# Two score regions for a group of two pairs in place of three, the third score tile in two banks of the MoE pool

## Chip, cores and metric

One core of one Trainium2 chip. The metric is the device time in microseconds (us) of one execution; every ratio compares fast runs alone (an execution over 1.5% above the fastest of its kernel counts as slow); medians and ranges are of all runs. "Span" is the profiled time from the first to the last instruction, some 2 us less than the time. Data are bf16 on chip, with float32 inputs, outputs and PSUM sums.

## The reference, cut to what matters

```python
# q, k, v: (8 batches, 8 heads, 576 positions, 64)
scores = (q @ k.transpose(0, 1, 3, 2)) / 8
scores = where(pos_i // 64 >= pos_j // 64, scores, -1e9)   # blockwise causal
attn = softmax(scores) @ v
x = attn.transpose(0, 2, 1, 3).reshape(4608, 512)
return maximum(x @ w1, x @ w2) @ w_out                      # d_ff = 1024
```

Two heads are a *pair* (32 in all), two pairs a *group* (16).

## The kernel before: the parts that matter

The program is written by hand in order, engine by engine. TensorE works on 128 rows of its array for the hidden matmuls (`ps_h`), the output matmuls (`ps_y`) and attention times values (`ps_o`), and on 64 rows for transposes and scores. A *region* is a stretch of 64-row work between stretches of 128-row work. TensorE's results land in the tiles of the PSUM pools, which the program lays out in *banks*: a bank here is the room of one `ps_m` tile of 128x512 float32. A tile's bank is used again once VectorE or ScalarE has copied the tile out (*evicted* it): at 24.33 us of the trace before, the first transpose into `ps_xo`, whose bank held the first `ps_kT` tile, starts 0.05 us after VectorE's copy of that tile has ended. The pools take eight banks: `ps_s` has two tiles of two banks for scores, `ps_m` four tiles of one bank for all else. It is called the MoE pool after the feed-forward part, whose first two products are the *hidden* matmuls and whose last one is the *output*; a *unit* is what fills and empties one tile of output, or a pair of hidden tiles.

```python
ps_s = ctx.enter_context(tc.tile_pool(name="ps_s", bufs=2, space=bass.MemoryType.PSUM))
ps_m = ctx.enter_context(tc.tile_pool(name="ps_m", bufs=4, space=bass.MemoryType.PSUM))

def h_unit(i, f):                    # 4 matmuls into each of two banks, then a maximum
    ...
    for w_sb in (w1_sb, w2_sb):
        pt = ps_m.tile([P, SPAN], FP32, name="ps_h", tag="m")
        for c in range(NDM):
            nc.tensor.matmul(pt[:, :w], w_sb[:, c, f * P:(f + 1) * P], xT[:, c, t0:t0 + w], ...)
            if c == NDM - 1:
                if not ph:
                    nc.vector.tensor_copy(out=h1[:, :w], in_=pt[:, :w])
                else:
                    nc.vector.tensor_max(g[:, f, m:m + w], h1[:, :w], pt[:, :w])
    ...
def transposes(nm, g, copies):       # two banks of ps_m, emptied by VectorE and ScalarE
    pts = [ps_m.tile([P, RPP, NP], BF16, name=f"ps_{nm}T", tag="m") for _ in range(2)]
    ...
def tile_0(p):                       # one of three score tiles of a pair, one exp
    u = ps_s.tile([P, 2, 512], FP32, name="ps_s", tag="s")
    scores(p, u, 0, 0, 0, 512)
    return lambda: (exp(p, u, 512, 0), mask(p, 0))
    ...
def x_out(g, t0=0, t1=NCH):          # transposes a group's x through two banks of ps_m
    pe = ps_m.tile([P, 2, n, BLK], BF16, name="ps_xe", tag="m")
    po = ps_m.tile([P, 2, n_odd, BLK], BF16, name="ps_xo", tag="m")
    ...
    nc.vector.tensor_copy(out=dst[:, :, :, 0], in_=pe[:])
    nc.vector.tensor_copy(out=dst[:, :, :n_odd, 1], in_=po[:])
    ...
for g in range(GPB, NG):             # fill(n): the next n hidden or output matmuls
    a, b = 2 * g, 2 * g + 1
    if x_due:
        x_out(x_due.pop())
    region(tile_0(a), tile_1(a))
    ...
    for p, tiles in ((a, lambda: (tile_2(a), tile_0(b))), (b, lambda: (tile_1(b), tile_2(b)))):
        fill(hi)
        av_with(p - LAG, lo)
        copy_out = t_pair(p)         # q's transposes of the next group with a, k's with b
        outs = tiles()
        copy_out()
        region(*outs)
        ...
```

The softmax here doesn't subtract the row's maximum and nothing guards it: scores larger than these inputs give would overflow.

## Time and profile before

| | before |
|---|---|
| time, median of 3 runs | 283.12 us (282.26 to 705.16; the last is not a fast run) |
| span, granted clock | 280.4 us, 1.000 |
| busy: TensorE, VectorE, ScalarE, GpSimd | 96, 66, 50, 38% |
| regions in a steady group, row-size changes in all | 3, 122 |
| steady group, between the starts of two x transposes | 15.0 us |

For later comparison I split the trace where each group's x transposes begin. For each stretch, *content* is the TensorE work that no wait explains: each 128-row matmul at the spacing seen when nothing waits (0.216 us for 512 columns), two 64-row ones on different halves of the array side by side, 0.094 us for each change of row size (92 to 97 ns in the steady groups). The *remainder* is the length less the content. A steady group before has 14.76 us of content and 0.25 of remainder.

### The profile page before, as it was taken

Reading aid. Unit: us, or ns where it says so; the run is one execution under the profiler, and the core shown is the slowest. Engines: PE = TensorE matmul, PEld = TensorE weight load, DVE = VectorE, ACT = ScalarE, POOL = GpSimd, SP = SyncE. Lnnn points to the kernel's source line nnn. Section 1 sums busy time; section 2 is a strip of 40 time slices with the busy share of each in tenths; the row PEclk is TensorE's granted clock in tenths of the full one; section 3 lists DMA queues with packets and bytes.
Section 4 is the critical chain, followed back from the end, with each engine's and each line's share of the span. In section 5 each row is a group of like instructions: output and inputs, shape, how many; then the busy total and the mean of one; then the engine's idle time right before and its main releaser. Section 6 shows DMA issues by size and latency. Waiting matters only on the chain.

```text
span 280.4 us, 7767 instructions
## 1 busy us (share of the span) xinstructions
PE 269.3 (96%) x3208; PEld 151.5 (54%) x3253; DVE 185.7 (66%) x386; ACT 139.6 (50%) x194; POOL 107.7 (38%) x271
## 2 busy tenths in 40 slices
PE   7699999999999999999999999999999999999995
PEld 2356766655556455555555554646455644444543
DVE  5967879668887676767667576757655766365430
ACT  3786577667664664655647374664653000100112
POOL 2996446764654625164344625371120000000000
PEclk9999999999999999999999999999999999999999
DMA  7999999979934994479266866175301111111114
GB/s 261 263 219 220 187 244 273 250 148 189 210 42 153 154 156 78 178 82 239 49 208 77 219 75 196 52 81 50 67 5 49 49 54 40 39 75 40 73 41 150
DMA packets 55940, 36.68 MB, mean 131 GB/s; under 512 B 38752, under 2 KB 43232, under 8 KB 55904
## 3 DMA queue, kind: packets, MB, share of 16 engines
q0 software_dynamic: 41728, 7.87, 35.0%
q1 hardware_dynamic: 13760, 27.66, 28.8%
q10 hardware_dynamic: 416, 0.66, 0.7%
q8 instruction: 25, 0.41, 0.6%
q14 instruction: 11, 0.09, 0.1%
HBM read 34.60 MB, written 9.44 MB: 157 GB/s over the span
## 4 chain that ended last, share of the span: by engine, by line
PE 91%; DMA 4%; issue 2%; ACT 1%; DVE 1%; POOL 0%; ACTq 0%
PE ps_h L197 43%; PE ps_y L215 22%; PE ps_o L429 11%; PE ps_s L321 8%; DMA vv<-in_v_dram 2%; PE ps_xe L451 2%; PE ps_qT L303 2%; DMA qraw<-in_q_dram 2%; PE ps_kT L303 2%; ACT aT L345 1%; PE ps_s L339 1%; PE ps_y L231 1%; PE ps_w L292 1%; DVE g L206 0%; POOL vv L133 0%
## 5 line engine op out<-in xcount | busy, mean ns | idle before, releaser
L197 PE MATMUL ps_h<-xT,w_sb 128*128 128x512 bf16 (+3 forms) x605 | 136.2, 357 | 1.7 <-issue 0.3
L345 ACT ACTIVATE aT<-ps_s 128x1024 bf16<-128x1024 f32 (+2 forms) x100 | 96.2, 996 | 17.2 <-PE ps_s L321 16.2
L197 PEld LDWEIGHTS <-w_sb 128*128 128x128 bf16 x640 | 57.8, 98 | 57.4 <-issue 8.1
L204 DVE CAST h<-ps_h 128x512 bf16<-128x512 f32 (+3 forms) x80 | 50.9, 637 | 28.9 <-PE ps_h L197 26.7
L215 PE MATMUL ps_y<-wo_sb,g 128*128 128x512 bf16 x273 | 65.5, 379 | 2.1 <-PE ps_s L321 1.3
L206 DVE TENSOR_TENSOR g<-h,ps_h 128x512 bf16<-128x512 bf16 (+3 forms) x80 | 50.6, 632 | 12.0 <-PE ps_h L197 10.5
L350 POOL MEMSET aT<- 64x128 bf16 x124 | 22.3, 199 | 92.7 <-ACT aT L345 91.3
L221 ACT COPY y<-ps_y 128x512 f32<-128x512 f32 x31 | 18.1, 584 | 70.3 <-PE ps_y L215 56.5
L429 PEld LDWEIGHTS <-aT 128*128 128x128 bf16 x960 | 37.3, 98 | 14.1 <-issue 1.3
L215 PEld LDWEIGHTS <-g 128*128 128x128 bf16 x280 | 26.8, 98 | 30.4 <-issue 1.1
L429 PE MATMUL ps_o<-vv,aT 128*128 128x65 bf16 x960 | 39.9, 194 | 0.3 <-DMA vv<-in_v_dram 0.3
L133 POOL DMA_DIRECT2D vv<-in_v_dram x40 | 33.7, 847 | 0.5
L436 DVE TENSOR_TENSOR xp<-ps_o,rec 128x256 bf16<-128x256 f32 (+1 forms) x64 | 31.4, 491 | 2.2
L321 PE MATMUL ps_s<-qT,kT 64*128 64x64 bf16 (+6 forms) x344 | 31.6, 279 | 1.1 <-ACT kT L310 0.7
L435 DVE RECIPROCAL rec<-ps_o 128x4 f32<-128x4 f32 (+1 forms) x64 | 12.0, 188 | 20.6 <-PE ps_o L429 18.9
L310 ACT COPY qT<-ps_qT 128x576 bf16<-128x576 bf16 x15 | 9.6, 638 | 29.4 <-PE ps_qT L303 29.4
L187 POOL COPY g<-g 128x512 bf16<-128x512 bf16 x8 | 4.9, 611 | 38.3 <-DVE g L206 38.2
L129 POOL CAST kn<-kraw 128x1152 bf16<-128x1152 f32 x15 | 17.3, 1151 | 5.2 <-DMA kraw<-in_k_dram 5.1
L129 POOL CAST qn<-qraw 128x1152 bf16<-128x1152 f32 (+1 forms) x15 | 16.5, 1099 | 7.0 <-DMA qraw<-in_q_dram 6.9
L456 DVE COPY xT<-ps_xe 128x640 bf16<-128x640 bf16 (+2 forms) x18 | 8.2, 453 | 15.7 <-PE ps_xe L451 14.9
L310 ACT COPY kT<-ps_kT 128x576 bf16<-128x576 bf16 x15 | 9.6, 638 | 15.0 <-PE ps_kT L303 15.0
L321 PEld LDWEIGHTS <-kT 64*128 64x128 bf16 x344 | 13.2, 95 | 6.6 <-issue 2.8
(44 smaller groups left out, 144.5 us busy)
## 6 DMA issues: line engine op xcount, KB each, us to landing
qraw<-in_q_dram SPq DMA_DIRECT2D x16, 576.0 KB, 4.1
out_dram<-y SPq DMA_DIRECT2D x35, 256.0 KB, 2.1
kraw<-in_k_dram SPq DMA_DIRECT2D x15, 576.0 KB, 5.4
vv<-in_v_dram POOLq DMA_DIRECT2D x32, 128.0 KB, 5.3
w_sb<-in_moe_w_dram POOLq DMA_DIRECT2D x4, 256.0 KB, 6.6
w_sb<-in_moe_w_dram POOLq DMA_DIRECT2D x2, 512.0 KB, 10.7
wo_sb<-in_moe_w_out_dram POOLq DMA_DIRECT2D x2, 512.0 KB, 11.8
kraw<-in_k_dram ACTq DMA_DIRECT2D x1, 576.0 KB, 5.4
```

Source lines behind the costliest of these rows:

```text
L129: copy(out=n[:, j0:j1], in_=t[:, j0:j1])
L133: nc.gpsimd.dma_start(out=vv_r[b % NV][P - rows:, c, :, :D], in_=v[b, :, c * P:c * P + rows, :].rearrange("h p d -> p h d"),)
L197: nc.tensor.matmul(pt[:, :w], w_sb[:, c, f * P:(f + 1) * P], xT[:, c, t0:t0 + w], start=(c == 0), stop=(c == NDM - 1),)
L204: nc.vector.tensor_copy(out=h1[:, :w], in_=pt[:, :w])
L206: nc.vector.tensor_max(g[:, f, m:m + w], h1[:, :w], pt[:, :w])
L215: nc.tensor.matmul(py[:], g[:, f, s * P:(s + 1) * P], wo_sb[:, f, :], start=(f == 0), stop=(f == NFF - 1),)
L310: copies[i](out=t[:, :S].rearrange("q (p j) -> q p j", j=RPP), in_=pts[i].rearrange("q j p -> q p j"),)
L321: nc.tensor.matmul(ps[:, hh, col:col + w], kT[r, k0:k0 + P], qT[r, q0:q0 + w], start=True, stop=True,)
L345: nc.scalar.activation(out=aT_r[p % NA][:, :, a0:a0 + w], in_=ps[:, :, :w], func=AF.Exp, scale=scale,)
L350: (eng or nc.gpsimd).memset(aT_r[p % NA][BLK:, :, a0:a0 + BLK], 0.0)
L429: nc.tensor.matmul(po[:, gi, hh, :], a[:, hh, a0:a0 + P], vv[:, c, h0 + 2 * hh, :], start=(mm == 0), stop=(mm == n_mm - 1),)
L436: nc.vector.tensor_mul(xp[:, ts[0]:ts[0] + n, :, p % 2], po[:, :, :, :D], rec[:, :n].to_broadcast([P, n, 2, D]),)
```

## The change

The intent is to save a third of the switches: the two pairs of a group get one region each, with all three score tiles. As `ps_s` holds two tiles, the third lies in two banks of the MoE pool and takes two exps of 512. q's transposes of the next group move into the first region, and `fill` can run on to the end of a unit, so that no bank is half filled when a region begins.

```diff
+    def tile_0m(p):
+        us = [ps_m.tile([P, 512], FP32, name="ps_s0", tag="m") for _ in range(2)]
+        for hh in range(2):
+            ...                      # one matmul of 512 columns into each
+        def out():
+            for hh in range(2):
+                nc.scalar.activation(
+                    out=aT_r[p % NA][:, hh, :512], in_=us[hh][:], func=AF.Exp, scale=scale)
+            mask(p, 0)
+        return out
...
-        region(tile_0(a), tile_1(a))
-        for p, tiles in ((a, lambda: (tile_2(a), tile_0(b))), (b, lambda: (tile_1(b), tile_2(b)))):
-            fill(hi)
...
+        for p in (a, b):
+            if p == a and x_due:
+                x_out(x_due.pop())
+                n = fill_of(g)
+            if p == a:
+                out1 = tile_1(a)
+                out0 = tile_0m(a)
+                out2 = tile_2(a)
+                copy_out = t_pair(a)
+                out0()
+                out1()
+                copy_out()
+                out2()
+            else:
+                copy_out = t_pair(b)
+                out1 = tile_1(b)
+                out0 = tile_0m(b)
+                out2 = tile_2(b)
+                ...
```

More of the change, by code (lines that the diff above doesn't have):

```diff
@@ L270 @@
     steps = [(u, need, cost) for u, need, cost, n in units for _ in range(n)]
+    inside = [j % (NDM if n > NFF or n == 2 * NDM and u.__name__ == "h_unit" else NFF) > 0
+              for u, _, _, n in units for j in range(n)]
     at = [0]
@@ L279, in ready, with fill @@
         return int(total)
-    def fill(n):
-        while n > 0 and at[0] < len(steps) and steps[at[0]][1] <= done_tokens[0]:
+    def fill(n, whole=False):
+        while at[0] < len(steps) and steps[at[0]][1] <= done_tokens[0]:
+            if n <= 0 and not (whole and inside[at[0]]):
+                break
             u, _, cost = steps[at[0]]
@@ L331, in pad_keys @@
         )
+    def tile_0m(p):
+        us = [ps_m.tile([P, 512], FP32, name="ps_s0", tag="m") for _ in range(2)]
+        for hh in range(2):
+            r = slice(hh * D, (hh + 1) * D)
+            nc.tensor.matmul(
+                us[hh][:], kT_r[p % NT][r, :P], qT_r[p % NT][r, :512], start=True, stop=True)
+        def out():
[4 more added lines that the diff above has]
+        return out
     def corner_scores(p, ps, col):
@@ L590 @@
         a, b = 2 * g, 2 * g + 1
-        if x_due:
-            x_out(x_due.pop())
         n = fill_of(g)
-        region(tile_0(a), tile_1(a))
-        if g == GPB:
-            av(3, [2, 3, 4])
-            fill(5)
-            x_out(1, 2, NCH)
-            n = fill_of(g)
-        lo, hi = max(3, n // 18), n * 2 // 9
-        for p, tiles in ((a, lambda: (tile_2(a), tile_0(b))), (b, lambda: (tile_1(b), tile_2(b)))):
-            fill(hi)
+        fill(0, True)
+        for p in (a, b):
[16 more added lines that the diff above has]
+                out2 = tile_2(b)
+                copy_out()
+                out1()
+                out0()
+                out2()
+                if g + 1 < NG:
+                    pad_keys(p + 1)
+                    pad_keys(p + 2)
+            pool_work(p)
+            if g == GPB and p == a:
+                av(3, [2, 3, 4])
+                fill(5)
+                x_out(1, 2, NCH)
+                n = fill_of(g)
+            lo = max(3, n // 18)
+            hi = max(0, n // 2 - lo)
             if g > GPB:
+                fill(hi * 3 // 5)
                 av_with(p - LAG, lo)
+                fill(hi - hi * 3 // 5, True)
             else:
-                fill(lo)
-            copy_out = t_pair(p)
-            outs = tiles()
-            copy_out()
-            region(*outs)
-            if p % 2 and g + 1 < NG:
-                pad_keys(p + 1)
-                pad_keys(p + 2)
-            pool_work(p)
+                fill(lo + hi, True)
         if g > GPB:
             x_due.append(g - 1)
-        fill(n - 2 * (lo + hi))
     for p in range(NPAIR - LAG, NPAIR):
```

## The prediction

> **What bounds the kernel now.** I read the page's busy shares and the line of the chain first, then the waits of TensorE, then the timeline of one group in the steady stretch, engine by engine.
>
> ```profile
> PE 269.3 (96%) x3208; PEld 151.5 (54%) x3253; DVE 185.7 (66%) x386; ACT 139.6 (50%) x194; POOL 107.7 (38%) x271
> PE 91%; DMA 4%; issue 2%; ACT 1%; DVE 1%; POOL 0%; ACTq 0%
> ```
>
> TensorE is busy 96% of the 280.4 us span and makes 91% of the chain that ended last. So anything that TensorE waits for adds to the time, and only less TensorE time can shorten it. The waits of TensorE between 85 and 202 us, where most groups lie:
>
> ```profile
> PE ps_y L215 <- PE ps_s L321: 1.3, 8, 0.2
> ```
>
> Nothing but 1.3 us, and its releaser is TensorE itself (a matmul record is missing before each). There is no wait on another engine to remove. What is left is the cost inside TensorE's own stream. The timeline of one region, 64-row matmuls (transposes and scores) between 128-row ones:
>
> ```profile
> 119.90 0.90 PE L429 MATMUL ps_o<-vv,aT 128*128 128x65 bf16 x24
> 120.74 0.44 PE L303 MATMUL ps_kT<-ident,kn 64*128 64x64 bf16 x18
> 121.01 0.38 PE L321 MATMUL ps_s<-qT,kT 64*128 64x64 bf16 x4
> 121.23 0.22 PE L339 MATMUL ps_s<-qT,kz 64*128 64x64 bf16 x4
> 121.28 0.36 PE L321 MATMUL ps_s<-qT,kT 64*128 64x320 bf16 x4
> 121.57 2.76 PE L197 MATMUL ps_h<-xT,w_sb 128*128 128x512 bf16 x11
> ```
>
> Attention-value matmuls start every 29.5 ns, but from the last of them to the first 64-row transpose are 124 ns: 94 ns extra. From the last 64-row score (128 columns, 56 ns) to the first 128-row matmul are 149 ns: 93 ns extra. Every change of row size in the steady groups shows 92 to 97 ns. VectorE in the same group, one hidden unit's two evictions:
>
> ```profile
> 123.51 0.69 DVE L204 CAST h<-ps_h 128x512 bf16<-128x512 f32 x1 [0.18 <-PE ps_h L197]
> 124.37 0.69 DVE L206 TENSOR_TENSOR g<-h,ps_h 128x512 bf16<-128x512 bf16 x1 [0.17 <-PE ps_h L197]
> ```
>
> Each starts 0.416 us after the start of the last 512-column matmul of its bank and takes 0.69. The reader is to see that a PSUM bank comes free 1.1 us after its last matmul started, while such a matmul holds TensorE for only 0.216. And from the groups by form, x's two copies out of PSUM:
>
> ```profile
> L456 DVE COPY xT<-ps_xe 128x640 bf16<-128x640 bf16 x14 | 6.9, 491 | 15.4 <-PE ps_xe L451 14.9
> L457 DVE COPY xT<-ps_xo 128x512 bf16<-128x512 bf16 x14 | 5.8, 415 | 0.0
> ```
>
> Last, the first group, whose inputs are still arriving (GpSimd's cast of q, then TensorE's scores and the transposes that use this cast):
>
> ```profile
> 29.60 1.15 POOL L129 CAST qn<-qraw 128x1152 bf16<-128x1152 f32 x1 [2.44 <-DMA qraw<-in_q_dram]
> ...
> 27.06 0.61 PE L321 MATMUL ps_s<-qT,kT 64*128 64x512 bf16 x6
> ...
> 31.98 0.44 PE L303 MATMUL ps_qT<-ident,qn 64*128 64x64 bf16 x18
> ```
>
> [...] The exps' 1026 ns (1024 elements) and 489 ns (384) give 0.84 per element and 167 fixed, near enough.
>
> **The change, part by part.** (1) Two 64-row regions in a group instead of three. Counting row-size changes in the built programs' order: 122 before, 94 after, 28 fewer (two in each of 14 groups). 28 x 0.094 = 2.6 us saved, all on TensorE. (2) The exp of the third tile is split in two of 512: by the fit above 0.167 + 512 x 0.84 = 0.60 us each, 1.19 instead of 1.03. 28 times 0.17 us is 5 us on ScalarE, which is 50% busy: beside other work, 0. (3) Matmuls, transposes and casts stay the same in number. (4) What binds: banks. The MoE pool has four. A first region of a group now takes xe, xo and the two halves of the third tile, all four banks, and then two more for the q transposes, which reuse xe's and xo's. A second region takes two for the k transposes and two for the tile: again all four. So the bank of the last hidden matmuls before the region is always among them; in the built program the second half of the tile lies in the bank that the last tensor_max reads. Before, a region took two, and the newest was never among them.
>
> Time from the start of the last 512-column matmul before a region. That bank is free at 0.416 + 0.687 + 0.054 = 1.16 us (0.054: end of a VectorE copy to the start of a matmul that waited for it, at 24.3 us of the trace). First region: 0.216 matmul + 0.095 switch + 0.251 x transposes + 0.218 tile 1 = 0.78: wait of 0.38. Then 0.216 tile 0, 0.25 tile 2: at 1.62 the q transposes want both x banks. VectorE, in order, does the max to 1.10, xe to 1.51, xo to 1.84 (each overlaps the one before by 0.083); bank free at 1.90: a further 0.27. Together 0.65 us. Second region: 0.216 + 0.095 + 0.265 k transposes + 0.218 tile 1 = 0.79: wait of 0.38, and no second one.
>
> Eleven groups have the full first region: 11 x 0.65 = 7.2. The last group's first region has no q transposes: 0.38. Eleven second regions at 512 columns: 4.2. Two at 320 columns: free at 0.88 against 0.71, 0.3 together. The last group's second region and the first regions of the first two groups find older banks: 0. Sum 12.0 us.
>
> (5) The q transposes of the next group move from the middle of a group to its first region. In the first group they follow tiles 1, 0 and 2, at about 27.3 + 0.7 = 28.0 us, but the cast ends at 29.60 + 1.15 = 30.75 and its DMA does not depend on the change: 2.9 us of waiting. In the second group the cast stands behind the masks, key pads and exps of the region before; from the row durations it ends near 42.9 with transposes wanted near 41.8: 1.2. Perhaps 0.3 in the fourth. Sum 4.4. In later groups I get the cast done some 2 us before its use.
>
> Sum: 283.1 - 2.6 + 12.0 + 4.4 = 296.9. I take 296, as small waits may overlap.
>
> **Rivals.** (a) Only the switches count: 280.5 us, 0.9% faster. For it: TensorE has no waits now, and 66% of VectorE looks like slack. Against it: an average share doesn't say when a bank is free, and the 1.1 us latency is seen in every unit. (b) Only bank waits, no early cast waits (the DMA lands sooner or other work moves ahead): 292.5. Against it: the built order of GpSimd up to that cast is unchanged. (c) Bank waits half as long, for instance because a unit that ends in a first half, or a y, is evicted differently: 289 to 291 with the casts. The y copy on ScalarE takes 0.58, a little less than VectorE's 0.69, so there is little in that. [...] (e) ScalarE becomes the bound: three tiles of a pair need about 1.03 + 1.19 + 1.03 + 0.27 + a 0.64 copy = 4.2 us in a half group of some 7.5; no.
>
> **Range and chances.** (a) would need both calculated waits to be absent, against two durations seen in every group: 0.01 for faster. Within 2% (up to 288.8) needs less than half of the waits: 0.07. Slower: 0.92. The range runs from rival (b) with somewhat shorter waits, 290, [...].
>
> **What would show it.** Switches: two fewer per group, each still 92 to 97 ns. Bank waits: TensorE's waits list rows of the third tile (ps_s0) released by VectorE's max, some 0.38 us each and about 23 of them, and of ps_qT released by the copy of xo, some 0.27 each and 11; steady groups grow from 15.0 to about 15.8 us. Cast waits: ps_qT released by GpSimd's qn, one near 2.9 and one near 1.2 us. ScalarE up by some 5 us in busy time, with no TensorE wait on an exp. The tail after the last group keeps its length. I would be wrong if the second half of the tile started at once after tile 1, or if the groups shrank by 0.19 us; or if a wait on an exp or on a mask stood in their place.

The sum is 283.1 - 2.6 + 12.0 + 4.4 = 296.9 us, put at 296. Cut are a paragraph that rested on rules which no trace here shows (its last sentence, the fit of the exps that part 2 uses, stays) and rival (d), on the clock, which was not in the sum. The upper end of the range, 300, allowed for that rival. Part 4 needs one thing, that a score tile waits until its banks are evicted; what the trace before shows of it is the wait at 24.33 us above.

## More of the kernel before

The prediction shows and reads the page's lines. The page also gives the granted clock in 40 slices, nine tenths or more in all of them:

```profile
PEclk9999999999999999999999999999999999999999
```

## The result, and the profile after

The changed kernel takes 296.85 us (median of 4 runs, 295.96 to 297.08) against 283.18 of the kernel before (median of 4, measured with it; one of these, 705.16, is not a fast run). Ratio 1.0488, 95% interval 1.0452 to 1.0524: slower by 4.9%. Ratios here are the mean time of one kernel's fast runs over that of the other's fast runs of the same rounds, so not quite the ratio of the medians. The span went from 280.4 to 295.0 us. The page's busy shares, the first line of the chain that ended last, and the clock, after:

```profile
PE 282.6 (96%) x3253; PEld 152.4 (52%) x3253; DVE 186.7 (63%) x386; ACT 139.6 (47%) x222; POOL 107.4 (36%) x271
...
PEclk9999799999999999999999999999999999999999
...
PE 82%; DMA 6%; DVE 5%; POOL 3%; ACT 2%; issue 1%; POOLq 0%; ACTq 0%
```

TensorE is still "96% busy", with 13.3 us more busy time for the same matmuls. (45 of their records are missing in the trace before; a run of the same matmuls with all records, the split exp below, shows 273.8, so some 9 us are real.) That share misleads: waiting for a bank is in part booked as busy (the pair of matmuls of a third tile below has 0.70 us of busy time, an unstalled pair 0.38). The chain tells it better: TensorE's part fell from 91 to 82%, and VectorE, GpSimd and a DMA came in. One digit of the clock, slice 5, fell to 7.

TensorE's waits after, longest first (in total, times, longest, us):

```profile
PE ps_qT L307 <- POOL qn L129: 3.7, 3, 2.9
PE ps_w L296 <- DVE zeros L157: 1.2, 1, 1.2
PE ps_s L325 <- ACT kT L314: 0.7, 1, 0.7
```

The cast waits are there: 2.89 us in the first group, at 31.20 us of the trace, and twice some 0.4 later. The other two rows are the prologue's, as before. No row names the new score tile. Its waits show in the timeline of a first region of a steady group, TensorE then VectorE (start, duration, engine, line; a bracket gives idle time and what ended it):

```profile
123.42 0.70 PE L342 MATMUL ps_s<-qT,kT 64*128 64x512 bf16 x2
...
124.14 0.19 PE L307 MATMUL ps_qT<-ident,qn 64*128 64x64 bf16 x1
...
124.47 0.42 PE L307 MATMUL ps_qT<-ident,qn 64*128 64x64 bf16 x17
124.83 1.25 PE L197 MATMUL ps_h<-xT,w_sb 128*128 128x512 bf16 x5
```

```profile
123.00 0.69 DVE L206 TENSOR_TENSOR g<-h,ps_h 128x512 bf16<-128x512 bf16 x1 [0.17 <-PE ps_h L197]
123.61 0.48 DVE L475 COPY xT<-ps_xe 128x640 bf16<-128x640 bf16 x1
124.01 0.41 DVE L476 COPY xT<-ps_xo 128x512 bf16<-128x512 bf16 x1
```

The first q transpose starts at 124.14, the other 17 from 124.47: 0.05 us after VectorE's copy of `ps_xo` ended (124.42). The two matmuls of the tile take 0.70 us together, where an unstalled pair takes 0.38 (at 27.68 us of this trace), because the second stands until VectorE's maximum has emptied its bank (123.69). The chain in the same stretch says it in a row:

```profile
121.24 1.74 PE ps_h L197 x8
122.98 0.02 issue
123.00 0.69 DVE g L206
123.69 0.40 DVE xT L475
124.09 0.34 DVE xT L476
124.43 0.04 issue
124.47 0.42 PE ps_qT L307 x17
```

For 1.4 us in each first region the kernel now runs at the pace of VectorE's three evictions. From the first x transpose to the next hidden matmul are 1.93 us, where the parts that the prediction uses, with 0.26 for q's transposes and 0.09 for the switch, give 1.29: a wait of 0.63. The second region takes 1.40 against 1.04: a wait of 0.36. There too it is the tile's second matmul, which starts 0.36 us after the first:

```profile
115.78 0.73 PE L342 MATMUL ps_s<-qT,kT 64*128 64x512 bf16 x2
```

The whole account of TensorE, in stretches between x transposes (lengths and content in us):

| stretch | remainder before | after | difference |
|---|---|---|---|
| first group with the new form (24 to 35 us of the trace after) | 0.63 | 5.17 | +4.5 |
| next (35 to 56 us) | 0.85 | 2.59 | +1.7 |
| eleven groups up to 217 us; a steady one 0.25 to 1.16 | 2.7 | 13.3 | +10.5 |
| last group | 0.24 | 0.54 | +0.3 |
| prologue and tail | 7.2 | 7.4 | +0.2 |
| content of everything | 267.3 | 264.7 | -2.6 |

The last column sums to the 14.6 us of the spans. The switches gave what they promised, 2.6 us. The remainder took 17.2 back: waits, and 1.7 us of half clock (below).

The 1.7 us of the second stretch are five waits: 0.44 for a cast, 0.16 and 0.49 for the maximum in two second regions, and 0.34 and 0.31 of hidden matmuls behind ScalarE. These two start 0.05 us after ScalarE's copy of q (ends at 46.51) and 0.05 us after the second exp of the new tile (ends at 52.11). So the new form also holds banks too long for the work that follows a region.

The first stretch holds more than the 2.89 us of waiting. These are windows of the trace after: length, then busy time of TensorE, its weight loads, VectorE, ScalarE and GpSimd, then the granted clock, the DMA share and the GB/s:

```profile
29.00:32.00 3.00, 0.80 (x29) 0.76 (x30) 0.33 (x1) 1.47 (x3) 1.15 (x1) 0.97 1.66 261
32.00:34.00 2.00, 2.00 (x24) 1.60 (x22) 1.38 (x4) 1.54 (x3) 1.57 (x4) 0.50 2.01 96
34.00:36.00 2.00, 2.00 (x21) 1.35 (x20) 1.20 (x5) 0.00 (x0) 1.73 (x6) 0.70 1.29 120
```

After the standstill the clock was granted at half for a while: 0.03 x 3 + 0.50 x 2 + 0.30 x 2 = 1.7 us lost. Asked more finely, the trace has a clock of 1.00 from 31.20, when TensorE has work again, to 31.80, then 0.50 for 3.42 us, then 1.00. Hidden matmuls of 256 columns started every 213 ns there, and every 109 later.

### The profile page after: what moved, and what is told of

Its sections match the earlier page's. It is cut to its first block, busy times and chain, and to the rows that moved or that the text cites. A ratio compares the mean times of both kernels' runs of the same rounds, so it can differ in the third digit from the quotient of the medians.

```text
span 295.0 us, 7891 instructions
## 1 busy us (share of the span) xinstructions
PE 282.6 (96%) x3253; PEld 152.4 (52%) x3253; DVE 186.7 (63%) x386; ACT 139.6 (47%) x222; POOL 107.4 (36%) x271
## 4 chain that ended last, share of the span: by engine, by line
PE 82%; DMA 6%; DVE 5%; POOL 3%; ACT 2%; issue 1%; POOLq 0%; ACTq 0%
PE ps_h L197 42%; PE ps_y L215 20%; PE ps_o L448 9%; DMA qraw<-in_q_dram 4%; PE ps_s L325 3%; DVE g L206 2%; DMA vv<-in_v_dram 2%; PE ps_s L342 2%; PE ps_qT L307 2%; PE ps_kT L307 2%; DVE xT L475 1%; DVE xT L476 1%; POOL vv L133 1%; ACT aT L347 1%; POOL qn L129 1%
## 5 line engine op out<-in xcount | busy, mean ns | idle before, releaser
L197 PE MATMUL ps_h<-xT,w_sb 128*128 128x512 bf16 (+3 forms) x640 | 138.9, 360 | 0.5 <-ACT qT L314 0.2
L197 PEld LDWEIGHTS <-w_sb 128*128 128x128 bf16 x640 | 59.2, 98 | 57.7 <-issue 3.4
L364 ACT ACTIVATE aT<-ps_s 128x1024 bf16<-128x1024 f32 (+2 forms) x72 | 71.5, 1000 | 7.4 <-PE ps_s L325 7.3
L215 PE MATMUL ps_y<-wo_sb,g 128*128 128x512 bf16 x280 | 71.9, 379 | 0.1
L347 ACT ACTIVATE aT<-ps_s 128x512 bf16<-128x512 f32 x56 | 30.5, 603 | 28.2 <-PE ps_s L342 28.2
L448 PE MATMUL ps_o<-vv,aT 128*128 128x65 bf16 x960 | 40.6, 195 | 0.3 <-DMA vv<-in_v_dram 0.2
L215 PEld LDWEIGHTS <-g 128*128 128x128 bf16 x280 | 24.6, 98 | 23.4 <-issue 0.4
L325 PE MATMUL ps_s<-qT,kT 64*128 64x320 bf16 (+5 forms) x288 | 31.6, 260 | 0.9 <-ACT kT L314 0.7
L314 DVE COPY qT<-ps_qT 128x576 bf16<-128x576 bf16 x17 | 12.9, 757 | 11.3 <-PE ps_qT L307 11.2
L342 PE MATMUL ps_s<-qT,kT 64*128 64x512 bf16 x56 | 18.6, 374 | 0.1
```

The costliest lines, as they stand in the source:

```text
L215: nc.tensor.matmul(py[:], g[:, f, s * P:(s + 1) * P], wo_sb[:, f, :], start=(f == 0), stop=(f == NFF - 1),)
L325: nc.tensor.matmul(ps[:, hh, col:col + w], kT[r, k0:k0 + P], qT[r, q0:q0 + w], start=True, stop=True,)
L342: nc.tensor.matmul(us[hh][:], kT_r[p % NT][r, :P], qT_r[p % NT][r, :512], start=True, stop=True)
L347: nc.scalar.activation(out=aT_r[p % NA][:, hh, :512], in_=us[hh][:], func=AF.Exp, scale=scale)
L364: nc.scalar.activation(out=aT_r[p % NA][:, :, a0:a0 + w], in_=ps[:, :, :w], func=AF.Exp, scale=scale,)
L448: nc.tensor.matmul(po[:, gi, hh, :], a[:, hh, a0:a0 + P], vv[:, c, h0 + 2 * hh, :], start=(mm == 0), stop=(mm == n_mm - 1),)
```

## The experiments

Theory: waits for PSUM banks (0.63 and 0.36 us in each steady group), the early casts and the clock after them are the whole loss. Rivals: the split exps, or ScalarE as the bound; switches that cost something else than 0.094 us; the two-region form as such. The kernel before took 282.36 us in the first four runs (median of 7), 282.69 in the next three (of 7) and 282.95 in the last two (of 9).

**q's transposes late in the first two groups.** All else as in the changed kernel.

```diff
-                copy_out = t_pair(a)
+                late = g < GPB + 2
+                copy_out = (lambda: None) if late else t_pair(a)
...
+                if p == a and late:
+                    t_pair(a)()          # a region of their own, half way on
```

> The changed kernel, but in its first two groups the q transposes stand in a short region of their own some units later, near where they stood before; all later groups unchanged. Theory (early cast waits plus a clock dip that the first wait brings on): the 2.9 us wait on GpSimd's cast, the 0.44 us one and about 1.6 us of half clock go, 4 switches of 0.094 come: 296.9 - 4.6 = about 292.3 us, and no slow-clock stretch near 32 us. Rival (the loss is only bank waits and the early wait would turn up elsewhere, for instance at the next transfer): 296 to 297.

291.82 us (ratio 1.0313, interval 1.0255 to 1.0371; one run of four, 296.18, was slow and is left out of the ratio), as expected. In the trace the clock was 1.00 throughout, the remainder of the first stretch 0.63 us as in the kernel before, and the steady groups kept their 15.73. So the early casts and the clock behind them cost 5 us, net of two more regions.

**Tile 0 last in its region.** The second half of tile 0 then wants its bank 0.25 us later.

```diff
-                out0 = tile_0m(a)
                 out2 = tile_2(a)
+                out0 = tile_0m(a)       # and the same for b
```

> The changed kernel with the two-bank tile issued as the last of the three score tiles instead of the second, so it is wanted 0.25 us later. Theory (wait for the eviction of the newest bank): in second regions the wait shrinks from 0.36 to about 0.11 us, in first regions nothing is gained, as the q transposes still wait for xo's copy: 13 x 0.25 = 3.2 us less, about 293.7 us; steady group 15.73 to about 15.48 us. Rival (a fixed cost of a tile in two single banks, or of the split exp): no change, 296.9.

294.72 us (1.0414, 1.0367 to 1.0460), groups 15.585: half a hit. In the second region the tile's wait fell from 0.36 to 0.11 us, but 0.12 came back: the hidden matmul after the region wanted the bank of `ps_kT`, whose copy on ScalarE had not ended.

```profile
115.26 0.48 PE L342 MATMUL ps_s<-qT,kT 64*128 64x512 bf16 x2
115.78 1.02 PE L197 MATMUL ps_h<-xT,w_sb 128*128 128x512 bf16 x4
```

```profile
115.10 0.64 ACT L314 COPY kT<-ps_kT 128x576 bf16<-128x576 bf16 x1 [1.62 <-PE ps_kT L307]
```

The copy ends at 115.73 and the matmul starts at 115.78. All four banks are in use, so whatever the region leaves last is what the next unit waits for. The groups fell by 0.145 us, about what the second region gave (0.25 less 0.12); the first gave nothing, since q's transposes wait for `ps_xo` either way.

**A slower maximum, in both kernels.** A dummy read of 128 columns of the same bank stands ahead of each maximum. That it holds the bank some 0.2 us longer is an estimate: the maxima of 512 and 256 columns take 0.685 and 0.416 us in the trace before, which gives 0.28 for 128 columns, less 0.083 by which VectorE's copies of `ps_xe` and `ps_xo` overlap there. In the changed kernel the maximum then started 0.21 us after the read (at 125.42 and 125.21 us of that run's trace).

```diff
+    idle = wpool.tile([P, P], BF16, name="idle")
...
+                        nc.vector.tensor_copy(out=idle[:], in_=pt[:, :P])
                         nc.vector.tensor_max(g[:, f, m:m + w], h1[:, :w], pt[:, :w])
```

In the changed kernel:

> The changed kernel with one more VectorE copy of 128 columns out of the same bank ahead of each hidden unit's max: the bank comes free about 0.2 us later; nothing else is changed and results stay right. Theory: each of the two regions of a group waits about 0.2 us longer: 12 groups x 0.4 = 4 to 5 us, so 301 to 302; steady group 15.73 to about 16.13. Rival (the waits come from elsewhere): 296.9 within 0.5.

In the kernel before:

> The kernel before with the same added copy, as a control: its regions never take the newest bank and VectorE has slack. Theory: 283 to 284 us, steady group 15.0 to 15.1. If it slows by 4 us too, the added copy says nothing about the change.

300.55 us in the changed kernel (1.0629, 1.0579 to 1.0679), slightly under its range; groups grew by 0.39 us, to 16.12. In the kernel before 283.47 (1.0026, 0.9986 to 1.0065), groups unchanged at 15.0. The rows of the same 80 reads of 0.29 us sum to 23 us in each (VectorE's busy total, which counts overlaps once, grows by 13.5 in each); only where a region waits for the maximum does TensorE pay. In the changed kernel the waits are now long enough to be listed by name, the third tile behind `g`:

```profile
PE ps_s L344 <- DVE g L208: 1.8, 10, 0.2
```

**The split exp alone, in the kernel before.**

```diff
-        return lambda: (exp(p, u, 512, 0), mask(p, 0))
+        # two nc.scalar.activation of 512 elements, then the mask
```

> The kernel before with one part of the change alone: the exp of tile 0 is issued as two activations of 512 elements, as in the changed kernel, all banks and the order as before. My theory (the split costs ScalarE 0.17 us a tile, some 2.7 us where the steady tiles are counted, beside other work): 283 us, within 1 us of the kernel before, groups still 15.0 us, ScalarE busier by 2 to 5 us. Rival (ScalarE's longer exps hold up the attention-value matmuls or the score pool, and this is part of the loss): 285 or more, with waits of TensorE on exps.

283.26 us (1.0002, 0.9949 to 1.0056): nothing. The exps' rows grew from 96.2 to 69.1 + 30.4 = 99.5 us, ScalarE's busy time from 139.6 to 141.3, and the groups stayed at 15.0. That rival is out.

**More switches in the kernel before.** One hidden matmul between transposes and tiles cuts two of a group's regions in two.

```diff
             copy_out = t_pair(p)
+            fill(1)
             outs = tiles()
```

> The kernel before with two more score regions per group in place of fewer: one 512-column hidden matmul is put between the transposes and the tiles of a region, so 174 changes of row size instead of 122, all else as before. It doubles the cost that the change set out to save. My theory (0.094 us each, no more): 52 x 0.094 = 4.9 us, so 288 us, groups 15.35 us. Rival (a change costs more than the two gaps show, so that the saving was in truth larger than 2.6 us and the waits too): 291 or more. Rival (the gaps are hidden by something else): 283 to 284.

288.18 us (1.0183, 1.0133 to 1.0233; slower, though not surely by 2%): 52 more changes cost 5.2 us by the ratio, 0.10 each (0.07 to 0.13 by the interval). A steady group grew by 0.43 us, of which 0.38 are its four changes at 0.094. The size of the saving was right.

**A cure for every wait found.** To the late q and tile 0 last, this adds a shift of the hidden work, so that an output unit, which ScalarE empties, stands before a region and VectorE is free; and it shares the copies of `ps_xo` and `ps_kT` between VectorE and ScalarE.

```diff
+        for s, copy in ((0, dve), (1, act)):             # ps_xo
+            copy(out=dst[:, s, :n_odd, 1], in_=po[:, s])
...
+                    for copy, p0 in ((dve, 0), (act, NP // 2)):   # ps_kT
+                        copy(out=t[:, p0:p0 + NP // 2], ...)
...
+            if 6 < g < NG - 1:
+                n = 32 if (g, p) == (7, 14) else 48
```

> The changed kernel with each found wait answered: q's transposes of the first two groups late as in the run before; tile 0 last in its region; the hidden work shifted so that in groups 8 to 14 a region follows an output unit, whose bank ScalarE empties while VectorE is free; the copies of kT and of xo shared between VectorE and ScalarE. Two regions a group are kept. My theory (the loss is waits for banks and early casts, nothing else in the form with two regions): steady groups about 15.05 us against 15.73, the whole 284 to 287 us, so most of the loss is cured, and about nothing is gained on the kernel before, as 0.2 to 0.3 us a group stay for the copies of x and k. Rival (two regions cost in themselves, or ScalarE becomes the bound once it takes more copies): 290 or more with groups of 15.5. Were all waits gone, groups would be 14.8 and the whole 281.

298.89 us (1.0553, 1.0505 to 1.0602), groups 16.13: a clear miss, worse than the change itself. The trace shows why:

```profile
138.26 0.28 DVE L484 COPY xT<-ps_xo 128x256 bf16<-128x256 bf16 x1
```

```profile
138.62 0.37 ACT L484 COPY xT<-ps_xo 128x256 bf16<-128x256 bf16 x1 [0.56 <-DVE xT L484]
```

ScalarE stood idle for 0.56 us with its half ready, and began 0.09 us after VectorE's half had ended. Both halves are in one bank, and in this trace the second engine waits for the first: its idle time is put down to VectorE's half (`<-DVE xT L484`). I had overlooked that, and no run here tried an overlap. The bank came free at 138.99 us; one copy of 0.41 us on VectorE, as in the changed kernel, would have ended at about 138.67 (an estimate from the two traces). q's transposes stood 0.47 us here for ScalarE's half, and 4.7 us in ten groups.

**The same with each bank copied by one engine.** ScalarE takes the whole of `ps_xo`, VectorE the whole of `ps_xe`, and `ps_kT` is as in the change.

```diff
+        (act if g > 1 else dve)(out=dst[:, :, :n_odd, 1], in_=po[:])
```

> The cured kernel of the run before with the shared copies taken back: ScalarE copies the whole of xo (VectorE the whole of xe) and each copy of kT has one engine, as in the changed kernel; q late in the first two groups, tile 0 last and the shift of the hidden work stay. My theory now (two engines asked for halves of one bank go one after the other, so the halves made each bank free later; in the cured trace the ScalarE half began only after the VectorE half had ended, and the waits were 0.47 to 0.65 us on xo and 0.33 to 0.39 on kT): xo's bank is free 0.35 us earlier and kT's first 0.2 us earlier, groups 15.6 us instead of 16.13, the whole 290 to 291.5 us. Rival (ScalarE's added copies themselves are what costs, since they stand behind the output copy): 294 or more, groups 16.0.

290.65 us (1.0266, 1.0236 to 1.0296), groups 15.59: as expected, 8 us less than with the halves, although ScalarE's busy time is higher (146.3 us against 145.2). So it was the sharing of a bank, not the load on ScalarE. Nor was it that both engines write the same tile `xT`: here they do so at the same time, from two banks.

```profile
148.07 0.49 DVE L475 COPY xT<-ps_xe 128x640 bf16<-128x640 bf16 x1 [0.97 <-PE ps_xe L470]
```

```profile
148.19 0.59 ACT L476 COPY xT<-ps_xo 128x512 bf16<-128x512 bf16 x1
```

But the waits have only moved once more:

```profile
PE ps_h L197 <- ACT aT L347: 2.0, 10, 0.2
PE ps_h L197 <- ACT kT L314: 1.3, 8, 0.2
```

The hidden matmuls after a region now wait for the exp of the new tile, or for the copy of k. This was the best form with two regions that I ran, 2.7% slower than the kernel before.

**TensorE kept busy in the cast wait.** Twelve matmuls of zeros ahead of the first group's q transposes; their result is not used.

```diff
+                if g == GPB:
+                    warm_up(12)
                 copy_out = t_pair(a)
```

> The changed kernel with 12 matmuls of zeros (2.6 us) put ahead of the first group's q transposes, where TensorE stood still for 2.9 us on the cast; their result is not used. The cast wait stays, but TensorE is busy in it. My theory (the stretch at half clock just after, worth some 1.65 us, comes from the standstill): granted clock 1.00 between 31 and 36 us, hidden matmuls of 256 columns there every 109 ns instead of 213, the whole 295.2 us, the wait of q's transposes down to about 0.3 us. Rival (the clock falls for another cause there, such as what stands just before, or the fillers themselves delay things): 296.9 or more with 213 ns again.

The same windows in this run:

```profile
29.00:32.00 3.00, 3.00 (x52) 1.76 (x50) 0.75 (x1) 1.67 (x4) 1.15 (x1) 1.00 1.67 258
32.00:34.00 2.00, 2.00 (x27) 1.48 (x24) 1.77 (x7) 1.12 (x2) 1.27 (x4) 1.00 1.89 85
34.00:36.00 2.00, 2.00 (x21) 1.78 (x20) 1.79 (x7) 0.00 (x0) 1.96 (x6) 1.00 0.80 73
```

The clock stays at 1.00 and the hidden matmuls start every 109 ns. The stretch took 9.19 us instead of 10.86, and the profiled span 293.3 us instead of 295.0: 1.7 us, the expected gain (0.2 of the stretch's gain is that the cast came sooner after its start). The median, 296.07 us (1.0451, 1.0425 to 1.0478), stands 0.9 us above the expectation, and its interval overlaps that of the changed kernel's ratio, so the size rests on the trace. So in this kernel it was the idle TensorE that brought the half clock: with q's transposes starting at 30.78 us instead of 31.20, but TensorE busy until then, it doesn't come. Two more traces agree: they have a wait for the cast of 2.6 us (tile 0 last) and of 3.1 us (slower maximum in the changed kernel), and each has slice 5 of the page's clock at 7 and a mean clock of 0.994, as the changed kernel has. That it always comes is not shown: over the twelve executions of these three kernels the mean clock is 0.993 or 0.994 in nine, and 0.999 or 1.000 in three, the fastest of each kernel; no trace of those three is kept. With fillers none of five is under 0.998. With q late the slow run is at 0.994, also without a trace.

## Why the prediction was right, point by point

- **What binds: TensorE's own stream, no wait on another engine to remove.** Right. The slower maximum in the kernel before cost nothing.
- **Part 1, switches: 2.6 us saved.** Right: the content of a steady group fell from 14.76 to 14.57, and 52 added changes cost 0.10 us each.
- **Part 2, the split exp: beside other work.** Right; alone it changed nothing. The rows of the exps grew by 5.8 us in the changed kernel (96.2 to 71.5 + 30.5), but ScalarE's busy total did not (139.6 in both). That total counts the overlap of one activation with the next once, so "up by some 5 us in busy time" was wrong as a sign to look for.
- **Part 4, banks: 0.65 and 0.38 us in each full group, 12.0 in sum.** Right in mechanism and nearly in size: 0.63 and 0.36 in the trace. The eleven groups from 56 to 217 us lost 10.5 us of remainder and the last one 0.3, 10.8 together. Some 0.5 of it is in one group only, with one wait on a cast and one on VectorE's scaling of x. The two second regions in the second stretch lost 0.65, where 0.3 was expected, so banks came to some 11.0 of 12.0. Not foreseen were the 0.65 us of hidden matmuls behind ScalarE in the second stretch, one of them on an exp, where the prediction had expected no such wait.
- **Part 5, early casts: 2.9 + 1.2 + 0.3.** The first was 2.89 (the prediction's own figures, 30.75 - 28.0, give 2.75). The second measured 0.44: in the trace the cast ended at 44.52 and the transposes were wanted at 44.14, so both came later than I had put them (42.9 and 41.8), the transposes by more. A third of 0.4 came in a later group. Sum 3.7 instead of 4.4.
- **The clock: not in the sum.** A loss came, of 1.7 us (3.42 us at 0.50 after the 2.89 us wait). The trace before could not give a figure for it: its clock is 1.00 in mean and nine tenths or more in every slice. That the sum hit the result to a tenth is partly luck: the waits alone took 15.5 us (17.2 less 1.7) where 16.4 were expected, and the two profiled executions lie 14.6 us apart where the medians lie 13.7 apart.
- **What would show it.** Wrong in form for the banks: I expected rows for the third tile in TensorE's list of waits. Waits of 0.3 us behind a running stream are booked as busy time there; the timeline and the chain show them. Once they had been made longer, they appeared under the name `ps_s` of the new tile. The tail did not keep its length either: from the last x transposes to the last matmul it fell from 50.7 to 49.0 us, because 1.7 us of matmuls now run earlier; its remainder stayed.

That an optimal two-region kernel cannot win is not shown. What is shown: the saving in switches is 0.19 us in a steady group, the waits of the change 0.91, and three reshufflings left at least 0.77 (15.59 - 14.57 - 0.25).

## What to carry to other kernels

Merging stretches of work to save a fixed cost also merges their demand on buffers: count the banks that the merged stretch takes, and if it takes all of them, the newest bank's eviction latency (here 0.416 + 0.69 + 0.05 = 1.16 us from the start of its last matmul) is on the path each time, as it was here with waits of 0.63 and 0.36 us in a steady group. Here each cure of one wait also uncovered another. When an engine's busy time grows with the same instructions (here TensorE's, by some 9 us), look for waits in the timeline and the chain, not in its list of waits. To free a bank sooner, giving each engine a whole bank did better here than giving it half of one: 290.65 us against 298.89.
